# Q loaded in 1 KB runs, and the query order restored by the masking multiply

## The chip, the cores and the metric

One core of one Trainium2 chip. The metric is the device time of one execution in microseconds (us). Each kernel was executed several times; the profile shows one of these executions. A run is called fast or slow by its time and its granted TensorE clock; ratios and intervals below use fast runs alone.

## The reference

Sliding-window causal attention (8 batches, 8 heads, 576 tokens, head size 64, window 64), followed by a gated two-layer network on the 4608 tokens (512 to 2048 to 512):

```python
scores = q @ k.T / sqrt(64)                       # per batch and head
mask   = (rel >= 0) & (rel < 64)                  # rel = query position - key position
attn   = softmax(where(mask, scores, -1e9))
x      = (attn @ v) as [tokens, heads * 64]
h      = x @ w_in
out    = (h * clip(h + 3, 0, 6) / 6) @ w_out
```

q, k and v are fp32 in DRAM, about 0.1 in size. The scores are so small that the softmax is nearly uniform over the window.

## The kernel before

Short names: PV is the product of the probabilities and V, K^T and x^T are transposes that a DMA makes (of K, and of the attention's result x), an `hT` bank is a piece of PSUM that holds one matmul group's result. The code is shortened; `...` marks what is left out.

The work is cut into stages of about 32 us. In stage T the TensorE does the two network layers of 512 tokens (`s1`, then `s2`); between their matmul groups it does the attention of a later batch. A batch has four pairs of heads `g`. For one pair:

```python
def load_blocks(t, src, b, kbs, tail=0):          # token s0 + p on partition p: 256 B runs
    for kb in kbs:
        ...
        nc.sync.dma_start(out=t[p0:p0+ss, kb, :, :],
                          in_=src[b, :, s0:s0+ss, :].rearrange("h s d -> s h d"))

def load_for_dma(b):                              # batches 2 to 7: q, k, v alike
    for n, src in (("qst", q), ("kst", k), ("vst", v)):
        t = stage.tile([P, KB, H, D], F32, name=n, tag=n)
        ins += load_blocks(t, src, b, range(KB), SR if src is v else 0)
...   # GpSimd casts to bf16 (qn, kn, V), then a DMA transpose gives QT, KT [d, token]

def scores(bt, g, u, ...):                        # st: PSUM, keys on partitions
    nc.tensor.matmul(st[:, h, o0:o0+n], lhsT=KT[..., k0:k0+P], rhs=QT[..., q0:q0+n])   # 192 queries per block
    # later: Exp on the ScalarE, PSUM -> SBUF bf16
    nc.scalar.activation(out=pT[:, :, 2*u:2*u+2, 0:QW], in_=st[...], func=EXP, scale=scale)

def masked(bt, g):                                # VectorE, in place, 2 * 4 * 192 = 1536 elements
    nc.vector.tensor_tensor(out=pT[:, :, :, 0:QW], in0=pT[:, :, :, 0:QW], in1=mask, op=MULT)
...   # PV matmuls into two hT banks of PSUM, then reciprocal and multiply (VectorE): opg
```

The VectorE runs in order. Besides the multiply it has the gate of each of the 16 matmul groups of `s1` (`gT`, 0.69 us), which frees the group's PSUM bank, and the normalisation of the PV result (`rec`, `opg`), which frees the two `hT` banks. From batch 3 on, the first two multiplies of a batch stand among the gates:

```python
p1 = {10: [f(SS, 0)], 14: [f(SS, 1)]}             # SS: scores, Exp, multiply of a pair
p2 = {0: [f(SS, 2)], 1: [f(N_, 0)], 3: [f(SS, 3), f(xt_dma, 0)], 4: [f(N_, 1)],
      ..., 7: [f(N_, 2)], ..., 10: [f(N_, 3)], 12: [f(X_, 3)]}   # N_: PV and normalisation
```

The softmax here doesn't subtract the row's maximum and nothing guards it: scores larger than these inputs give would overflow.

## Time and profile before

| | before |
|---|---|
| time, median of 3 | 319.54 us (319.47 to 319.94) |
| span of the profiled run | 317.6 us, granted clock 1.0 |
| TensorE busy | 300.8 us |
| VectorE busy | 173.9 us |
| masking multiply | shortest 947 ns, median 958 ns |

The head of the profile's page. Each engine's busy time, its share of the span and its instructions:

```profile
PE 300.8 (95%) x2131; PEld 149.5 (47%) x2167; DVE 173.9 (55%) x331; ACT 177.9 (56%) x265; POOL 85.7 (27%) x131
```

The waits of the TensorE: engine, line, what was written, who ended the wait, us in total, times, longest.

```profile
PE st L347 <- DMA KT<-kn: 2.4, 2, 2.0
...
PE st L466 <- DMA xT<-opg: 1.0, 1, 1.0
```

So the TensorE is the bound. Of its 16.8 us of idle time (317.6 - 300.8), 3.4 us are waits for transfers in the middle of the kernel; a lighter Q load can win these.

Groups of the page: line, engine, operation, operands, shapes, count, then busy us and mean ns, idle time before.

```profile
L365 DVE TENSOR_TENSOR pT<-pT,mask 128x1536 bf16<-128x1536 bf16 x28 | 28.1, 1004 | 23.0 <-ACT pT L355 23.0
...
L252 POOL CAST qn<-qst 128x512 bf16<-128x512 f32 x24 | 16.1, 712 | 74.1 <-DMA qst<-in_q_dram 59.7
```

The timeline of the VectorE and then of the TensorE in one stage (start, duration, engine, line, operation):

```profile
142.15 0.96 DVE L365 TENSOR_TENSOR pT<-pT,mask 128x1536 bf16<-128x1536 bf16 x1 [0.72 <-ACT pT L355]
143.03 0.68 DVE L474 SCALAR_TENSOR_TENSOR gT<-t,hT 128x512 bf16<-128x512 bf16 x1
...
146.15 0.96 DVE L365 TENSOR_TENSOR pT<-pT,mask 128x1536 bf16<-128x1536 bf16 x1 [0.65 <-ACT pT L355]
147.03 0.68 DVE L474 SCALAR_TENSOR_TENSOR gT<-t,hT 128x512 bf16<-128x512 bf16 x1
```

```profile
144.36 1.04 PE L466 MATMUL hT<-xT,win 128*128 128x512 bf16 x4
...
147.76 0.22 PE L377 MATMUL hT<-V,pT 128*128 128x65 bf16 x2
```

The last gate of the stage starts at 147.03 and ends at 147.71; the PV group that takes the bank it frees starts at 147.76. The engine that looks 45% idle has almost no slack here. Every delay of this gate is a delay of the TensorE.

### The profile page before, as it was taken

The page shows a single profiled execution, that of the slowest core. Times are in us where ns is not written, and L with a number is a line of the kernel's source. Part 1 is how long each engine was busy: PE and PEld are TensorE (multiplying, and loading weights), DVE is VectorE, ACT ScalarE, POOL GpSimd, SP SyncE. Part 2 cuts the span into 40 slices and gives each one's busy share as a digit, 9 for nine tenths or more (in the row PEclk, how much of TensorE's full clock was granted, in tenths as well). Part 3 has the DMA queues.
Part 4 walks back from the last instruction along what each step waited for, and adds up shares of the span by engine and source line. Part 5 has one row for each costly group of instructions (what it writes and reads, how often), then busy time and mean ns, then how long its engine had stood idle before and what let it go on. Part 6 is the DMA issues. An engine that isn't in the chain of part 4 may idle for free.

```text
span 317.6 us, 5604 instructions
## 1 busy us (share of the span) xinstructions
PE 300.8 (95%) x2131; PEld 149.5 (47%) x2167; DVE 173.9 (55%) x331; ACT 177.9 (56%) x265; POOL 85.7 (27%) x131
## 2 busy tenths in 40 slices
PE   8989799999999799899999999999999999999995
PEld 3454345544554355344544554445444544444442
DVE  4658643476636665277527853785378438406700
ACT  2748753387637771487258725872587347417711
POOL 5741805363045143305610650065000000000000
PEclk9999999999999999999999999999999999999999
DMA  8999999999799999999999998999800630010011
GB/s 211 237 173 253 238 199 205 204 184 248 158 208 209 270 215 205 191 254 204 195 257 210 207 184 208 211 201 185 204 34 2 122 75 0 28 73 33 0 68 66
DMA packets 150843, 52.64 MB, mean 166 GB/s; under 512 B 138272, under 2 KB 146464, under 8 KB 150816
## 3 DMA queue, kind: packets, MB, share of 16 engines
q1 hardware_dynamic: 146000, 46.77, 72.7%
q0 software_dynamic: 4544, 5.24, 9.5%
q8 instruction: 17, 0.28, 0.4%
q10 hardware_dynamic: 272, 0.26, 0.2%
q14 instruction: 10, 0.08, 0.1%
HBM read 36.70 MB, written 9.44 MB: 145 GB/s over the span
## 4 chain that ended last, share of the span: by engine, by line
PE 63%; DMA 21%; SPq 8%; POOL 3%; issue 2%; DVE 1%; ACT 1%; POOLq 0%
PE o L503 15%; PE acc L503 14%; PE hT L466 14%; PE acc L466 5%; PE o L466 5%; SPq L94 5%; DMA vst<-in_v_dram 4%; DMA kst<-in_k_dram 4%; DMA KT<-kn 4%; DMA qst<-in_q_dram 3%; PE st L466 3%; PE st L347 3%; DMA wout<-in_moe_w_out_dram 3%; DMA win<-in_moe_w_in_dram 3%; PE hT L377 1%
## 5 line engine op out<-in xcount | busy, mean ns | idle before, releaser
L466 PEld LDWEIGHTS <-win 128*128 128x128 bf16 x576 | 55.3, 98 | 67.2 <-issue 2.3
L503 PEld LDWEIGHTS <-gT 128*128 128x128 bf16 x576 | 52.9, 98 | 57.5 <-issue 0.6
L503 PE MATMUL o<-wout,gT 128*128 128x512 bf16 x274 | 67.5, 379 | 1.5 <-DMA wout<-in_moe_w_out_dram 0.7
L503 PE MATMUL acc<-wout,gT 128*128 128x512 bf16 x278 | 67.1, 379 | 0.7 <-issue 0.3
L466 PE MATMUL hT<-xT,win 128*128 128x512 bf16 x266 | 65.7, 379 | 0.3
L355 ACT ACTIVATE pT<-st 128x768 bf16<-128x768 f32 x64 | 48.9, 813 | 10.8 <-PE st L347 10.7
L473 ACT ACTIVATE t<-hT,half 128x512 bf16<-128x512 f32 x68 | 46.7, 690 | 9.6 <-PE hT L466 9.2
L474 DVE SCALAR_TENSOR_TENSOR gT<-t,hT 128x512 bf16<-128x512 bf16 x68 | 46.4, 685 | 9.4 <-ACT t L473 9.1
L474 DVE SCALAR_TENSOR_TENSOR gT<-t,st 128x512 bf16<-128x512 bf16 (+1 forms) x26 | 19.7, 768 | 52.9 <-ACT t L473 52.9
L365 DVE TENSOR_TENSOR pT<-pT,mask 128x1536 bf16<-128x1536 bf16 x28 | 28.1, 1004 | 23.0 <-ACT pT L355 23.0
L509 ACT COPY osb<-o 128x512 f32<-128x512 f32 x18 | 10.6, 586 | 46.2 <-PE o L503 46.2
L252 POOL CAST qn<-qst 128x512 bf16<-128x512 f32 x24 | 16.1, 712 | 74.1 <-DMA qst<-in_q_dram 59.7
L509 ACT COPY osb<-acc 128x512 f32<-128x512 f32 x18 | 10.6, 587 | 35.7 <-PE acc L503 33.7
L466 PE MATMUL st<-xT,win 128*128 128x512 bf16 x117 | 28.2, 379 | 1.7 <-DMA xT<-opg 1.0
L397 DVE TENSOR_TENSOR opg<-hT,rec 128x320 bf16<-128x320 f32 x56 | 27.5, 492 | 1.9
L466 PE MATMUL acc<-xT,win 128*128 128x512 bf16 x91 | 23.6, 379 | 0.1
L466 PE MATMUL o<-xT,win 128*128 128x512 bf16 x90 | 23.5, 379 | 0.1
L473 ACT ACTIVATE t<-st,half 128x512 bf16<-128x512 f32 (+1 forms) x26 | 19.4, 752 | 7.2 <-PE st L466 7.1
L377 PEld LDWEIGHTS <-pT 128*128 128x128 bf16 x256 | 17.8, 97 | 9.1 <-issue 1.4
L347 PE MATMUL st<-QT,KT 64*128 64x192 bf16 (+2 forms) x320 | 17.9, 229 | 4.2 <-DMA KT<-kn 2.4
L394 DVE RECIPROCAL rec<-hT 128x5 f32<-128x5 f32 x56 | 10.5, 188 | 20.0 <-PE hT L386 19.9
L243 POOL CAST V<-vst 128x512 bf16<-128x512 f32 (+1 forms) x14 | 16.4, 1168 | 17.4 <-DMA vst<-in_v_dram 17.0
(76 smaller groups left out, 269.2 us busy)
## 6 DMA issues: line engine op xcount, KB each, us to landing
out_dram<-osb SPq DMA_DIRECT2D x32, 256.0 KB, 2.4
qst<-in_q_dram SPq DMA_DIRECT2D x28, 256.0 KB, 4.7
kst<-in_k_dram SPq DMA_DIRECT2D x27, 256.0 KB, 5.4
vst<-in_v_dram SPq DMA_DIRECT2D x24, 256.0 KB, 5.1
vst<-in_v_dram SPq DMA_DIRECT2D x24, 128.0 KB, 4.1
win<-in_moe_w_in_dram POOLq DMA_DIRECT2D x4, 512.0 KB, 7.6
wout<-in_moe_w_out_dram POOLq DMA_DIRECT2D x4, 512.0 KB, 8.8
qst<-in_q_dram SPq DMA_DIRECT2D x2, 512.0 KB, 6.1
```

The lines of the kernel that those rows point to most:

```text
L243: copy(out=self.V[:, 0 : KB - 1, h0:h1, 0:D], in_=vst[:, 0 : KB - 1, h0:h1, :])
L252: pcopy(out=n[:, g, 0 : KB - 1, :, :].rearrange("p k h d -> p k (h d)"), in_=s[:, 0 : KB - 1, 2 * g : 2 * g + 2, :].rearrange("p k h d -> ...
L347: nc.tensor.matmul(st[:, h, o0 : o0 + n], lhsT=bt.KT[h * D : (h + 1) * D, g, k0 : k0 + P], rhs=bt.QT[h * D : (h + 1) * D, g, q0 : q0 + n], ...
L355: nc.scalar.activation(out=pT[:, :, 2 * u : 2 * u + 2, 0:QW], in_=st[:, :, 0:w].rearrange("p h (k w) -> p h k w", k=2), func=EXP, scale=scale,
L365: nc.vector.tensor_tensor(out=pT[:, :, :, 0:QW], in0=pT[:, :, :, 0:QW], in1=mask[:].rearrange("p (h k) w -> p h k w", h=2), op=MULT,)
L377: nc.tensor.matmul(ob, lhsT=pT[:, h, qb, 0:P], rhs=V[:, qb, 2 * g + h, :], start=True, stop=(qb == 0),)
L397: nc.vector.tensor_tensor(out=opgs[bt.b, g][:, :, h, :], in0=ov[:, :, 0:D], in1=rec[:].unsqueeze(2).to_broadcast([P, KB, D]), op=MULT,)
L466: nc.tensor.matmul(hT, lhsT=win16[:, g, fc * P : (fc + 1) * P], rhs=xT[:, g, t0 : t0 + TB], start=(g == 0), stop=(g == NG - 1),)
L473: nc.scalar.activation(out=t1[:], in_=hT, func=RELU, bias=half[:], scale=1.0 / 6.0)
L474: nc.vector.scalar_tensor_tensor(out=out, in0=t1[:], scalar=1.0, in1=hT, op0=MIN, op1=MULT,)
L503: nc.tensor.matmul(accs[ts], lhsT=gT[:, fc, ts * P : (ts + 1) * P], rhs=wout16[:, fc, :], start=(fc == 0), stop=(fc == NFC - 1),)
L509: nc.scalar.copy(out=osb[:], in_=accs[ts])
```

## The change

Q of batches 2 to 7 is loaded with four neighbouring tokens to a partition: runs of 1 KB in place of 256 B (the first 512 tokens; the last 64 are loaded as before). The transposed Q then comes with its queries in the order (j, s) for token 4 s + j. The score matmuls read it in four short runs and leave the scores in the order (j, s) too; the Exp writes them to a new tile `raw`; and the multiply, which has to read and write all of it anyway, writes its result at the place of token 4 s + j, that is 2-byte elements in steps of 8 B. The intent is to relieve the transfers and to get the reordering for nothing. In the shortened diffs, a pattern in quotes behind a tile stands for its `rearrange`.

```diff
 def load_for_dma(b):
+    for h0 in range(0, H, 4):
+        nc.sync.dma_start(out=qst[:, h0:h0+4, :],
+            in_=q[b, h0:h0+4, 0:SM, :].rearrange("h (p j) d -> p h (j d)", j=R))
+    nc.sync.dma_start(out=rst[0:SR, :, :], in_=q[b, :, SM:S, :].rearrange("h s d -> s h d"))
-    for n, src in (("qst", q), ("kst", k), ("vst", v)):
+    for n, src in (("kst", k), ("vst", v)):
 ...                                    # cast: qn in the order (j, h, d) of a partition's tokens
 def scores(...):                       # batches 2 to 7
+    matmul(st[...]"(j s) -> j s"[:, :, 0:n], lhsT=KT[...], rhs=QT[...]"(j s) -> j s"[:, :, s0:s0+n])
+    activation(out=raw[:, :, 2*u:2*u+2, :], in_=st[...], func=EXP, scale=scale)
 def masked(bt, g):
+    nc.vector.tensor_tensor(
+        out=pT[:].rearrange("p h k (s j) -> p (h k) j s", j=R)[:, :, :, 0 : QW // R],
+        in0=raws.pop((bt.b, g))[:].rearrange("p h k (j s) -> p (h k) j s", j=R),
+        in1=maskj[:], op=MULT)
```

More of the change, by code (lines that the diff above doesn't have):

```diff
@@ L56 @@
     stage = ctx.enter_context(tc.tile_pool(name="stage", bufs=1))
+    rawp = ctx.enter_context(tc.tile_pool(name="raw", bufs=2))
     small = ctx.enter_context(tc.tile_pool(name="small", bufs=4))
@@ L125, in load_for_dma @@
         sts, ins = [], []
-        for n, src in (("qst", q), ("kst", k), ("vst", v)):
+        qst = stage.tile([P, H, R * D], F32, name="qst", tag="qst")
+        rst = stage.tile([P, H, D], F32, name="rst", tag="rst")
+        for h0 in range(0, H, 4):
+            ins.append(nc.sync.dma_start(
+                out=qst[:, h0 : h0 + 4, :],
+                in_=q[b, h0 : h0 + 4, 0:SM, :].rearrange("h (p j) d -> p h (j d)", j=R),
+            ))
+        ins.append(nc.sync.dma_start(
+            out=rst[0:SR, :, :], in_=q[b, :, SM:S, :].rearrange("h s d -> s h d"),
+        ))
+        for n, src in (("kst", k), ("vst", v)):
             t = stage.tile([P, KB, H, D], F32, name=n, tag=n)
@@ L129, in load_for_dma @@
             sts.append(t)
-        return tuple(sts), ins
+        return ((qst, rst), *sts), ins
     ctx.enter_context(tc.manual_schedule())
@@ L216 @@
     mask = consts.tile([P, 2 * (KB - 1), QW], BF16, name="mask")
+    maskj = consts.tile([P, 2 * (KB - 1), R, QW // R], BF16, name="maskj")
+    raws = {}
     win16 = consts.tile([P, NG, FF], BF16, name="win16")
@@ L249, in cast_for_dma @@
         def cast_for_dma(self, st, which=(0, 1, 2)):
-            for n, s in [((qn_all, st[0]), (kn_all, st[1]))[i] for i in which if i < 2]:
+            for i in which:
+                if i > 1:
+                    continue
+                n = (qn_all, kn_all)[i]
                 for g in range(NG):
-                    pcopy(
-                        out=n[:, g, 0 : KB - 1, :, :].rearrange("p k h d -> p k (h d)"),
-                        in_=s[:, 0 : KB - 1, 2 * g : 2 * g + 2, :].rearrange("p k h d -> p k (h d)"),
-                    )
+                    if i:
+                        pcopy(
+                            out=n[:, g, 0 : KB - 1, :, :].rearrange("p k h d -> p k (h d)"),
+                            in_=st[1][:, 0 : KB - 1, 2 * g : 2 * g + 2, :].rearrange("p k h d -> p k (h d)"),
+                        )
+                    else:
+                        pcopy(
+                            out=n[:, g, 0 : KB - 1, :, :],
+                            in_=st[0][0][:, 2 * g : 2 * g + 2, :].rearrange("p h (j d) -> p j h d", j=R),
+                        )
+                rest = st[1][:SR, KB - 1, :, :] if i else st[0][1][:SR, :, :]
                 pcopy(
                     out=n[:SR, :, KB - 1, :, :].rearrange("p g h d -> p g (h d)"),
-                    in_=s[:SR, KB - 1, :, :].rearrange("p (g h) d -> p g (h d)", h=2),
+                    in_=rest.rearrange("p (g h) d -> p g (h d)", h=2),
                 )
@@ L340, in scores @@
                 )
+        if bt.b > 1:
+            QJ = QW // R
+            if u == 0:
+                raws[bt.b, g] = rawp.tile([P, 2, KB - 1, QW], BF16, name="raw")
+            for i in range(2):
+                for h in range(2):
+                    kb = 2 * u + i
+                    n = min(QJ, P - kb * P // R)
+                    nc.tensor.matmul(
+                        st[:, h, i * QW : (i + 1) * QW].rearrange("p (j s) -> p j s", j=R)[:, :, 0:n],
+                        lhsT=bt.KT[h * D : (h + 1) * D, g, kb * P : (kb + 1) * P],
+                        rhs=bt.QT[h * D : (h + 1) * D, g, 0:SM].rearrange("d (j s) -> d j s", j=R)[
+                            :, :, kb * P // R : kb * P // R + n
+                        ],
+                        start=True, stop=True,
+                    )
+            if u:
+                for h in range(2):
+                    nc.tensor.matmul(
+                        st[:, h, QW : 2 * QW].rearrange("p (j s) -> p j s", j=R)[:, :, P // R : QJ],
+                        lhsT=bt.KT[h * D : (h + 1) * D, g, S - P : S],
+                        rhs=bt.QT[h * D : (h + 1) * D, g, SM:S].rearrange("d (s j) -> d j s", j=R),
+                        start=True, stop=True,
+                    )
+            raw = raws[bt.b, g]
+            return lambda: nc.scalar.activation(
+                out=raw[:, :, 2 * u : 2 * u + 2, :],
+                in_=st[:, :, 0:w].rearrange("p h (k w) -> p h k w", k=2),
+                func=EXP, scale=scale,
+            )
         blocks = (
@@ L364, in masked @@
         pT = P_ring[(bt.b * NG + g) % NPT]
+        if bt.b > 1:
+            nc.vector.tensor_tensor(
+                out=pT[:].rearrange("p h k (s j) -> p (h k) j s", j=R)[:, :, :, 0 : QW // R],
+                in0=raws.pop((bt.b, g))[:].rearrange("p h k (j s) -> p (h k) j s", j=R),
+                in1=maskj[:], op=MULT,
+            )
+            return
         nc.vector.tensor_tensor(
@@ L746, in pieces @@
         return p1, p2
+    nc.vector.tensor_copy(out=maskj[:], in_=mask[:].rearrange("p n (s j) -> p n j s", j=R))
     bt2 = Batch(2)
```

## The prediction

> **What bounds the kernel now.** The TensorE. The page has it busy 300.8 of 317.6 us at full clock. In 8 us windows it idles about 0.05 us each from 136 us on. Its waits after 50 us add up to about 5 us; those that transfers end are K^T of batch 3 (2.0 us at 105 us, timeline), x^T of batch 3's last pair (1.0 us at 130 us) and K^T of batch 2 (0.4 us at 76 us). So a lighter Q load can win about 3.4 us.
>
> **What the change removes.** Q of six batches: 4096 runs of 256 B become 1024 runs of 1 KB per batch. In the sync queue's timeline the five Q issues of a batch take 4.2 to 6.0 us, and from 47 to 133 us the queue is never free. I estimate 1.5 to 2.5 us saved per batch; twice that is ahead of batch 3's K^T, which was 2.0 us late. All three waits should go: -3.4 us.
>
> **What it adds.** The masking multiply (24 of 28) writes 2-byte elements 8 bytes apart. The Trainium skill, "VectorE: DVE Perf Modes", "The perf-mode tier table", gives tensor_tensor in bf16 from SBUF 2x, and its section on that mode asks for step 1. The trace agrees: 1536 elements in 958 ns. At one element a cycle I estimate 1.75 us (gate ops in the trace: 512 elements 685 ns, 320 in 492 ns, slope 1.0 ns). +0.8 us each, 19 us of VectorE time, VectorE from 174 to about 194 us. Exp, GpSimd casts and score matmuls keep their durations.
>
> **How much is on the path.** Read in the timelines of the stage at 139 to 160 us, per stage of batches 3 to 7:
> - first multiply 0.8 longer: the four gates behind it slip, the bank that the last gate matmul group needs is freed 0.1 to 0.2 us late;
> - second multiply: the last gate of the stage ended 0.1 us before the second PV group of pair 0 took its bank; now it is about 0.7 us late;
> - fourth multiply: normalisation of pair 1 behind it is late for PV of pair 2 by about 0.4 us.
> Together about 1.2 us, five stages: +6 us. Batch 2 has slack: 0. The multiply has two SBUF inputs and already stretched to 1.36 us beside GpSimd casts; longer multiplies collide more: +0 to 1 us.
>
> Sum: 319.5 - 3.4 + 6 + 0.5 = 322.6 us. 80% range 318.3 to 331. Chances: faster by over 2% 0.02, within 2% 0.78, slower by over 2% 0.20.
>
> **What would show it.** Groups: the multiply at 1.7 to 1.8 us; q1 packets down by 18,400; VectorE busy up 19 to 20 us. Waits: TensorE no longer waits for K^T or x^T transfers (over 0.3 us), but for VectorE (gates releasing hT banks, reciprocal/normalisation) about 1.2 us in each of five stages, at the last gate group, PV of pair 0 and PV of pair 2. TensorE busy unchanged within 1 us.
>
> **What would make it wrong.** If strided 2-byte writes cost more than one cycle[...], the multiply takes 2.5 to 4 us, the time 335 or more; a memset of 40 elements 130 bytes apart took 92 ns against 59 ns for one, which speaks against it. If the multiply keeps the 2x rate, the time is 316. If the earlier transfers move GpSimd's 1.9 us V cast onto a multiply, stages lose more than I say.

## The result, and the profile after

| | before | after |
|---|---|---|
| time | 319.74 us median of 4 | 370.42 us median of 4 (368.04 to 373.66) |
| ratio of fast runs | | 1.154, 95% interval 1.144 to 1.164 |
| span, granted clock of the profiled run | 317.6 us, 1.0 | 371.9 us, 0.967 |
| TensorE busy | 300.8 us | 316.1 us |
| VectorE busy | 173.9 us | 241.1 us |
| masking multiply, batches 2 to 7 | 0.96 us | shortest 3.57, mean 3.92, longest 5.67 us |

A ratio here is the mean time of one kernel's fast runs over that of the other's of the same rounds, so not quite the ratio of the medians. The profiled run of after was its slowest (373.66 us); its fast runs were 368 to 371.7 us at a clock of 0.977 to 0.986. So its waits are read here, but its clock is a little lower than usual, and the fast profiles of e2 and e9 below are taken to confirm it.

The page of after, and the group of the multiply:

```profile
PE 316.1 (85%) x2131; PEld 152.6 (41%) x2167; DVE 241.1 (65%) x332; ACT 177.9 (48%) x265; POOL 120.6 (32%) x131
...
L419 DVE TENSOR_TENSOR pT<-raw,maskj 128x1536 bf16<-128x1536 bf16 x24 | 93.8, 3917 | 9.7 <-ACT raw L389 9.7
...
L274 POOL CAST qn<-qst 128x512 bf16<-128x512 f32 x24 | 20.8, 894 | 83.5 <-DMA qst<-in_q_dram 83.5
```

Waits of the TensorE:

```profile
PE hT L437 <- DVE gT L534: 12.2, 5, 2.9
PE hT L437 <- DVE opg L457: 12.2, 13, 2.6
PE hT L526 <- DVE gT L534: 9.6, 5, 2.1
PE hT L467 <- DVE opg L457: 3.6, 3, 1.7
...
PE hT L437 <- DVE pT L419: 1.4, 1, 1.4
...
PE st L372 <- DMA KT<-kn: 0.6, 1, 0.6
```

These five waits for the VectorE are 39.0 us. 34.0 us are in the stages of batches 3 to 7, at the kinds of place that the prediction named: the last gate group of a stage (L526) and the PV groups (L437). New are the transpose of the result (L467, 3.6 us) and the 1.4 us that end with the multiply itself: both are in the stage of batch 2, from 84 to 99 us, for which the prediction had 0. The transfer waits went from 3.4 us to 0.6. The packets of the hardware queue fell by 18,624 (146,000 to 127,376), as the prediction had it.

The span grew by 54.3 us: 39.0 us more idle TensorE, and 15.3 us more busy TensorE. About 10 us of the second part are the granted clock; what the other 5 us are was not taken apart (both traces have 2131 matmul records where e1 to e3 have 2167, so the sums are short by a little). The stretch of one stage, in windows of 4 us (PE, PEld, DVE, ACT and POOL busy, then PEclk, the DMA share and GB/s):

```profile
160.00:164.00 4.00, 3.13 (x22) 1.39 (x22) 3.57 (x6) 3.12 (x5) 3.04 (x5) 1.00 1.19 212
164.00:168.00 4.00, 1.20 (x18) 0.94 (x18) 4.00 (x3) 0.95 (x2) 4.00 (x3) 0.79 0.55 103
168.00:172.00 4.00, 3.95 (x18) 1.56 (x18) 4.00 (x1) 0.72 (x2) 3.94 (x2) 0.50 0.00 0
172.00:176.00 4.00, 3.81 (x29) 1.75 (x30) 3.91 (x6) 1.28 (x2) 1.66 (x2) 0.85 0.58 103
```

In the second window the TensorE was busy for 1.2 of 4 us, and in the third it ran at half clock. Over the whole span I sum busy time times (1 - clock) in such windows: 10.0 us for after, 0.0 for before. The Trainium skill, "TensorE: Matmul & The Clock Gate", "What's actually happening", says that the clock is halved after an idle window of about 3.4 us. This trace has half clock behind long waits, but the longest of its waits is 2.95 us, so none was as long as that window. Here there were two waits, of 2.05 us (to 160.84) and 2.63 us (to 167.23), with 3.8 us of work between them. The length of the waits does not decide it alone: one stage later two waits of 1.82 and 2.60 us (to 202.56 and 208.92) left the clock at 1.0, as the single 1.97 us wait of before did, while in e7 a single wait of 2.34 us was followed by half clock. No run here shows the rule.

The timeline of the VectorE in this stage, and the second PV group that waits for its gate:

```profile
163.00 3.66 DVE L419 TENSOR_TENSOR pT<-raw,maskj 128x1536 bf16<-128x1536 bf16 x1 [0.43 <-ACT raw L389]
166.46 0.72 DVE L534 SCALAR_TENSOR_TENSOR gT<-t,hT 128x512 bf16<-128x512 bf16 x1
167.11 5.66 DVE L419 TENSOR_TENSOR pT<-raw,maskj 128x1536 bf16<-128x1536 bf16 x1
```

```profile
167.23 0.27 PE L437 MATMUL hT<-V,pT 128*128 128x65 bf16 x2 [2.63 <-DVE gT L534]
```

It is the pair of lines shown of before at 147.03 and 147.76: gate, then PV. The gate is now 2.7 us late because the multiply in front of it takes 3.66 us in place of 0.96.

GpSimd at the same time:

```profile
161.51 5.44 POOL L269 CAST kn<-kst 128x512 bf16<-128x512 f32 x4 [0.96 <-DMA kst<-in_k_dram]
166.89 0.60 POOL L279 CAST kn<-kst 64x512 bf16<-64x512 f32 x1
167.45 1.89 POOL L256 CAST V<-vst 128x2048 bf16<-128x2048 f32 x1
169.40 3.65 POOL L257 CAST V<-vst 64x512 bf16<-64x512 f32 x1
```

Four K casts that take 0.61 us each by themselves took 5.44 us, the multiply at 167.11 took 2.1 us more than the shortest while the 1.89 us V cast ran, and the small V cast (0.61 us by itself) took 3.65 us and ended 0.3 us after that multiply. The Trainium skill, "SBUF — State Buffer", "Who interferes with whom", says that a VectorE instruction with two SBUF inputs and a GpSimd instruction that reads SBUF block each other, whichever is second. The trace agrees.

### The profile page after: what moved, and what is told of

Its sections match the earlier page's. It is cut to its first block, busy times and chain, and to the rows that moved or that the text cites. A ratio compares the mean times of both kernels' runs of the same rounds, so it can differ in the third digit from the quotient of the medians.

```text
span 371.9 us, 5575 instructions
## 1 busy us (share of the span) xinstructions
PE 316.1 (85%) x2131; PEld 152.6 (41%) x2167; DVE 241.1 (65%) x332; ACT 177.9 (48%) x265; POOL 120.6 (32%) x131
## 3 DMA queue, kind: packets, MB, share of 16 engines
q1 hardware_dynamic: 127376, 46.77, 58.3%
## 4 chain that ended last, share of the span: by engine, by line
PE 46%; DVE 25%; DMA 11%; ACT 8%; issue 5%; POOL 3%; SPq 1%; ACTq 0%; POOLq 0%
DVE pT L419 19%; PE o L563 11%; PE acc L563 11%; PE hT L526 8%; ACT raw L389 5%; PE st L526 4%; PE acc L526 4%; PE o L526 4%; DVE gT L534 3%; DVE opg L457 3%; DMA wout<-in_moe_w_out_dram 3%; DMA win<-in_moe_w_in_dram 2%; DMA kst<-in_k_dram 2%; ACT t L533 2%; DMA KT<-kn 2%
## 5 line engine op out<-in xcount | busy, mean ns | idle before, releaser
L419 DVE TENSOR_TENSOR pT<-raw,maskj 128x1536 bf16<-128x1536 bf16 x24 | 93.8, 3917 | 9.7 <-ACT raw L389 9.7
L526 PEld LDWEIGHTS <-win 128*128 128x128 bf16 x576 | 55.5, 98 | 76.8 <-issue 10.5
L563 PEld LDWEIGHTS <-gT 128*128 128x128 bf16 x576 | 55.0, 101 | 64.2 <-issue 11.1
L563 PE MATMUL o<-wout,gT 128*128 128x512 bf16 x274 | 74.4, 409 | 2.3 <-DMA wout<-in_moe_w_out_dram 1.0
L526 PE MATMUL hT<-xT,win 128*128 128x512 bf16 x266 | 65.6, 379 | 9.9 <-DVE gT L534 9.6
L563 PE MATMUL acc<-wout,gT 128*128 128x512 bf16 x278 | 69.4, 389 | 0.7 <-issue 0.3
L274 POOL CAST qn<-qst 128x512 bf16<-128x512 f32 x24 | 20.8, 894 | 83.5 <-DMA qst<-in_q_dram 83.5
L437 PE MATMUL hT<-V,pT 128*128 128x65 bf16 x224 | 18.4, 197 | 26.3 <-DVE gT L534 12.2
L389 ACT ACTIVATE raw<-st 128x768 bf16<-128x768 f32 x48 | 36.2, 814 | 4.4 <-PE st L372 4.4
L269 POOL CAST kn<-kst 128x512 bf16<-128x512 f32 x24 | 28.0, 1206 | 18.8 <-DMA kst<-in_k_dram 18.8
L437 PEld LDWEIGHTS <-pT 128*128 128x128 bf16 x256 | 17.9, 98 | 39.2 <-DVE opg L457 16.7
L569 ACT COPY osb<-acc 128x512 f32<-128x512 f32 x18 | 10.5, 586 | 44.5 <-PE acc L563 42.6
L526 PE MATMUL st<-xT,win 128*128 128x512 bf16 x117 | 28.1, 379 | 1.6 <-DMA win<-in_moe_w_in_dram 1.0
L526 PE MATMUL acc<-xT,win 128*128 128x512 bf16 x91 | 23.6, 379 | 0.1
L526 PE MATMUL o<-xT,win 128*128 128x512 bf16 x90 | 23.5, 379 | 0.1
```

The costliest lines, as they stand in the source:

```text
L269: pcopy(out=n[:, g, 0 : KB - 1, :, :].rearrange("p k h d -> p k (h d)"), in_=st[1][:, 0 : KB - 1, 2 * g : 2 * g + 2, :].rearrange("p k h d ...
L274: pcopy(out=n[:, g, 0 : KB - 1, :, :], in_=st[0][0][:, 2 * g : 2 * g + 2, :].rearrange("p h (j d) -> p j h d", j=R),)
L389: return lambda: nc.scalar.activation(out=raw[:, :, 2 * u : 2 * u + 2, :], in_=st[:, :, 0:w].rearrange("p h (k w) -> p h k w", k=2), func= ...
L419: nc.vector.tensor_tensor(out=pT[:].rearrange("p h k (s j) -> p (h k) j s", j=R)[:, :, :, 0 : QW // R], in0=raws.pop((bt.b, g))[:].rearran ...
L437: nc.tensor.matmul(ob, lhsT=pT[:, h, qb, 0:P], rhs=V[:, qb, 2 * g + h, :], start=True, stop=(qb == 0),)
L526: nc.tensor.matmul(hT, lhsT=win16[:, g, fc * P : (fc + 1) * P], rhs=xT[:, g, t0 : t0 + TB], start=(g == 0), stop=(g == NG - 1),)
```

## The experiments

My theory after the result (theory 1): the whole loss is the multiply's duration on the VectorE, from the strided write; the load, the matmuls and the new tile are innocent. Rivals: a part of it comes from moved transfers and casts or from the matmuls (A); the loss of two elements a cycle is enough by itself, with the collisions (B, D); any pattern that isn't innermost-dense costs as much (C).

### e1: the multiply writes densely

```diff
-    out=pT[:].rearrange("p h k (s j) -> p (h k) j s", j=R)[:, :, :, 0 : QW // R], ...
+    out=pT[:, :, :, 0:QW].rearrange("p h k w -> p (h k) w"),
+    in0=raw "p h k w -> p (h k) w", in1=maskj "p n j s -> p n (j s)"      # wrong order, on purpose
```

> The changed kernel with one edit: the multiply writes its result densely (query order not restored, so the result is wrong on purpose). Theory 1 (the whole loss is the multiply's duration on the VectorE): the multiply is back at 0.95 to 1.0 us, the GpSimd casts near 0.61 us, the TensorE waits for the VectorE gone, time 316 to 318 us, that is 1.5 to 3.5 us under the kernel before. Rival A (part of the loss is elsewhere: score matmuls that read four short runs, the extra tile between Exp and multiply, transfers or casts that now come at other times): the time stays above 325 us with the multiply at 1 us.

Measured: ratio to before 0.993 (interval 0.986 to 1.001). Two runs at a clock of 0.998 or more took 316.4 and 316.9 us; the other two, at 0.992 and 0.989, took 320.5 and 322.3 (the last is left out of the ratio). The profiled one, 320.5 us, has a dip of the clock near 42 us. The multiply, and the largest wait for the VectorE from 60 us on (1.6 us in all):

```profile
L419 DVE TENSOR_TENSOR pT<-raw,maskj x24: 957/959/2647, 80.0 to 248.9; 128x1536 bf16<-128x1536 bf16 x24
PE hT L437 <- DVE opg L457: 1.3, 3, 0.9
```

Rival A falls: with new load, new matmul patterns and new tile the loss is gone. The gain of 1.5 to 3.5 us that was expected is not clear of the noise in these runs. The wrong result was found by the check (the mask no longer fits).

### e2: the old load, the new multiply

```diff
-    (Q in 1 KB runs, cast in the order j h d)
+    (Q loaded and cast as before)              # scores, raw, strided multiply as after; wrong on purpose
```

> The changed kernel with Q loaded and cast as before (256 B runs); score matmuls, Exp, multiply with 8 B steps as after; wrong result on purpose, mask read from the unpermuted tile. Theory 1: 366 to 376 us, as the changed kernel, multiply 3.6 us in its shortest runs; the load takes part neither in the loss nor, now, in any gain, as the stages wait for the VectorE. Rival A (moved transfers and casts make the loss): 320 to 345 us.

Measured: ratio 1.167 (1.163 to 1.172), 372.9 to 374.8 us. Waits for the VectorE 42.6 us from 60 us on, clock 0.963; the multiply and the largest of the waits:

```profile
L398 DVE TENSOR_TENSOR pT<-raw,mask x24: 3569/3598/5589, 77.8 to 301.1; 128x1536 bf16<-128x1536 bf16 x24
PE hT L416 <- DVE gT L513: 15.1, 5, 4.4
```

So the loss is all there without the new load, and rival A falls again. e2 is 1.3% slower than after (1.167 against 1.154), which would mean that the new load still wins something, against the expectation; but the two ran on different chips and their intervals overlap, so this stays open. This is also a fast profile with the clock as low as in the one of after.

### e3: one element a cycle, no steps

```diff
+    mask32 = consts.tile([P, KB - 1, QW], F32)
-    (strided multiply with the bf16 mask)
+    nc.vector.tensor_tensor(out=pT[:, :, :, 0:QW], in0=raw[:],
+        in1=mask32[:].unsqueeze(1).to_broadcast([P, 2, KB - 1, QW]), op=MULT)   # wrong order, on purpose
```

> The changed kernel with a dense multiply whose mask is fp32 (result wrong on purpose): one element a cycle, no steps. This is the multiply that the prediction assumed. Theory 1: 1.75 us each, and, if the prediction's path was right (3.4 us won, 6 to 7 us lost), 321 to 325 us; if the stages have more slack than it read, 316 to 319. Rival B (one element a cycle is already enough for the measured loss, e.g. because of collisions with GpSimd): above 340 us.

This is the kernel that the prediction thought it was looking at. Measured: multiply shortest 1748 ns, median 1760; ratio 1.028 (1.023 to 1.033), 328.1 to 328.8 us in the three runs at a clock of 0.998 or more (330.8 us in the profiled one, at 0.992). So the estimate of 1.75 us for one element a cycle was right, and it is a loss of only 8 to 9 us. Rival B falls. But the time is also 6 us above the 322.6 that the prediction made of this duration; e8 takes that apart. The waits for the VectorE (8.5 us from 60 us on):

```profile
PE hT L436 <- DVE gT L533: 4.8, 5, 1.2
PE hT L436 <- DVE opg L456: 3.4, 9, 1.1
```

### e4: eight forms of the multiply in one kernel

```diff
+    v = ((bt.b - 2) * NG + g) % 8      # three multiplies of each form; wrong on purpose
+    0: dense    1: dense, fp32 mask
+    2, 3, 4, 5: out=pT "p h k (s j) -> p (h k) j s" with j = 2, 4, 8, 16   # steps of 4, 8, 16, 32 B
+    6: out dense, in0=raw "(j s) -> s j"     # read in steps of 96 B: restores the order
+    7: out dense, in0=raw "(s j) -> j s"     # read in steps of 8 B
```

> The changed kernel with eight forms of the multiply in turn, three of each (result wrong on purpose): dense; dense with fp32 mask; write steps of 4, 8, 16, 32 B; dense write with a read of one input in steps of 96 B (which restores the order); dense write with a read in steps of 8 B. Theory 1a (a step costs what the short run of 2-byte writes costs the memory port, over the loss of two elements a cycle): shortest dense 0.95, fp32 1.75, 4 B 1.75, 8 B 3.6, 16 and 32 B 3.6 to 4, read in steps of 96 B 2.5 to 3.9. Rival C (any pattern that isn't innermost-dense, or any pattern in short rows, costs 3.6 us): 4 B also 3.6, and the reads too. Rival D (only the loss of two elements a cycle plus contention): all 1.75.

Measured, in the order of the forms 0 to 7 (shortest/median/longest ns):

```profile
L429 DVE TENSOR_TENSOR pT<-raw,mask x3: 957/958/958, 77.9 to 239.0; 128x1536 bf16<-128x1536 bf16 x3
L431 DVE TENSOR_TENSOR pT<-raw,mask x3: 1759/1759/1760, 79.3 to 243.1; 128x1536 bf16<-128x1536 bf16 x3
L433 DVE TENSOR_TENSOR pT<-raw,mask x3: 1900/2241/2253, 82.4 to 245.3; 128x1536 bf16<-128x1536 bf16 x3
L435 DVE TENSOR_TENSOR pT<-raw,mask x3: 3957/4839/4874, 86.3 to 249.7; 128x1536 bf16<-128x1536 bf16 x3
L437 DVE TENSOR_TENSOR pT<-raw,mask x3: 6984/6986/6995, 107.9 to 276.7; 128x1536 bf16<-128x1536 bf16 x3
L439 DVE TENSOR_TENSOR pT<-raw,mask x3: 6639/6641/7128, 117.6 to 286.5; 128x1536 bf16<-128x1536 bf16 x3
L441 DVE TENSOR_TENSOR pT<-raw,mask x3: 2737/3391/5105, 125.1 to 293.5; 128x1536 bf16<-128x1536 bf16 x3
L447 DVE TENSOR_TENSOR pT<-raw,mask x3: 1749/1759/1759, 131.4 to 299.7; 128x1536 bf16<-128x1536 bf16 x3
```

The 8 B form fell beside GpSimd casts in all three places (two of them beside a V cast of 1.90 us); after and e2 have it at 3569 ns alone. Rivals C and D fall: a read in steps of 8 B takes 1.76 us, as the dense form with the fp32 mask does, while a write in steps of 8 B takes more than twice that. The rows get shorter as the steps of the writes get longer (96, 48, 24 and 12 elements), so the length of a row was not held; but the read in steps of 8 B has rows of 48 too, and rows of 12 took no longer than rows of 24. My own sizes for 16 and 32 B (3.6 to 4 us) were wrong by a factor of almost two, and 4 B took 1.90 us where I had 1.75.

Take 158 ns off (what the dense form leaves over 768 cycles at the 0.96 GHz that the Trainium skill, "VectorE: DVE Perf Modes", "Specifications", gives): the writes cost 1.09, 2.13, 4.27 and 4.05 cycles an element at steps of 4, 8, 16 and 32 B. At 4, 8 and 16 B, where four, two and one element fall into each 16 B of SBUF, that is 4.3 to 4.4 cycles for every 16 B touched; at 32 B it is 4.05. The numbers fit a cost for each 16 B piece written in part; no run here shows the mechanism.

### e5: four other places for the reordering

```diff
-    (raw tile and strided multiply)
+    multiply in place and dense; v = (bt.b + g) % 4 chooses where the order is restored:
+    0: activation(out=pT dense, in_=st "(j s) -> s j")     # Exp reads PSUM in steps of 192 B
+    1: activation(out=pT "(s j) -> j s", in_=st dense)     # Exp writes SBUF in steps of 8 B
+    2: matmul(out=st "(s j) -> j s", ...)                  # PSUM written in steps of 16 B
+    3: matmul(..., rhs=QT "(j s) -> s j")                  # moving operand in steps of 256 B
```

For an Exp in one instruction, pT was laid out as [u, h, k] and the PSUM blocks start at multiples of 256.

> The changed kernel with the multiply dense again (in place, two elements a cycle) and the query order restored at four other places in turn, six pairs each: (0) Exp reads PSUM in steps of 192 B and writes densely; (1) Exp reads densely and writes in steps of 8 B; (2) the score matmul writes PSUM in steps of 16 B; (3) the score matmul reads its moving operand in steps of 256 B. Right result by construction. If the 16 B line cost of the last runs holds for any engine that writes SBUF, (1) takes the Exp from 0.81 to over 1.7 us; if it is the VectorE's own, 0.81. (0): 0.81 if PSUM reads in steps are free, else 1 to 2 us. (2) and (3): a pair of ten score matmuls takes 0.5 us now; free means 0.5, a cost per element means 1 us and more. Whichever form leaves all four durations alone is the one for a whole kernel, at 316 to 317 us. Multiply 0.95 to 1.0 us in all.

Measured: the Exp of the forms 0 and 1, and the ten score matmuls of a pair with the plain pattern and in the forms 2 and 3:

```profile
L392 ACT ACTIVATE pT<-st x12: 802/811/817, 83.0 to 253.7; 128x768 bf16<-128x768 f32 x12
L397 ACT ACTIVATE pT<-st x12: 1876/1934/1983, 86.9 to 256.6; 128x768 bf16<-128x768 f32 x12
```

```profile
176.97 0.53 PE L383 MATMUL st<-QT,KT 64*128 64x192 bf16 x10
...
211.86 0.82 PE L385 MATMUL st<-QT,KT 64*128 64x192 bf16 x10
...
247.41 1.39 PE L387 MATMUL st<-QT,KT 64*128 64x192 bf16 x10
```

So this strided write to SBUF is dear on the ScalarE too (1.93 us against 0.81), and both TensorE forms cost time on the engine that bounds the kernel (0.82 to 0.90 us and 1.39 us for a pair, against 0.53). The Exp's strided read of PSUM costs nothing (0.81 us in both). (Single run, correct, 333 us: the four forms mixed.)

### e6 and e7: the free place, with the new and with the old load

e6 is form 0 of e5 for all pairs, with the multiply dense and in place. e7 is the same with Q loaded and cast as before (its query order is wrong).

> The changed kernel with the query order restored by the Exp, which reads PSUM in steps of 192 B, and the multiply dense and in place as before. Right result by construction. Theory 1: Exp 0.81 us, multiply 0.95 to 1.0 us where no cast collides, casts near 0.61 us; the TensorE waits for K^T and x^T transfers are gone; 315.5 to 317.5 us in runs at full clock, 1% faster than before (less in the mean if runs with a dip of the granted clock are among them). Rival: earlier transfers and casts collide with multiplies enough to give the 3 us back: 319 to 321 us.

Measured: ratio 0.993 (0.990 to 0.997), 317.2 to 319.5 us beside 319.5 to 322.9 for before on that chip. Exp 0.81 us, multiply median 959 ns; no wait for a transfer is left after 60 us. The two runs at full clock took 317.2 and 319.4 us, so only one of them is within the 315.5 to 317.5 us that I expected. 0.7% better than before is the best correct version found. Its correctness rests on the index maps and on the mask, since the check doesn't see the query order.

> The same kernel with Q loaded and cast as before the change (256 B runs), so the query order comes out wrong on purpose. It separates the load from the new layout of scores and probabilities. Theory 1 (the load is the whole gain): 319 to 320.5 us, with the TensorE waits for K^T and x^T transfers (2 us and 1 us) back. Rival (the new layout wins or loses by itself): over 1.5 us away from the kernel before.

Measured: ratio 1.002 (0.997 to 1.006). One wait for a transfer is back, for K^T of batch 3 (2.3 us); the one for x^T is not:

```profile
107.74 0.71 PE L363 MATMUL st<-QT,KT 64*128 64x192 bf16 x10 [2.34 <-DMA KT<-kn]
...
108.00:112.00 4.00, 4.00 (x19) 1.58 (x16) 1.65 (x2) 2.44 (x4) 0.00 (x0) 0.59 1.13 260
```

(The second line is the window behind that wait, in the columns used above: its granted clock is 0.59, and 0.50 from 108 to 110 us.) So the layout is neutral within the noise, and the new load is worth 0.8%, or 2.7 us: 1.0016 - 0.9932 = 0.0084, times 319.5. From the two intervals I estimate plus or minus 1.7 us.

### e8 and e9: without the casts

```diff
-    p1.setdefault(12 if T == 1 else 6, []).append(lambda bt=nxt, sts=sts: bt.cast_for_dma(sts))
```

This takes the GpSimd casts of batches 3 to 7 away, so that these use old data (wrong): e8 from e3, e9 from after.

> e3 (dense multiply with fp32 mask, 1.76 us) without the GpSimd casts of batches 3 to 7 (so those batches use old data: wrong on purpose, if the check can see it). Nothing is left on GpSimd that a multiply could collide with. If collisions with casts are what made e3 slower than the prediction's path said, all multiplies of batches 3 to 7 take 1.75 us, each stage waits 1.0 to 1.2 us for the VectorE as batch 7 did in e3, and the time falls from 328 to 322 to 325 us. If the path itself was read too short (refills of the TensorE, small waits), it stays at 327 or above.

Measured: all multiplies 1748 to 1759 ns; ratio 1.020 (1.016 to 1.024), 325.3 to 327.9 us. Neither of the two answers alone: the collisions are about 0.8% (1.028 - 1.020; 2.6 us, plus or minus 2 us by the two intervals, the two ratios being of different chips), and the path was read too short as well. Waits for the VectorE:

```profile
PE hT L436 <- DVE gT L533: 4.0, 5, 0.8
...
PE hT L436 <- DVE opg L456: 1.1, 5, 0.2
```

5.1 us in five stages, 1.0 each, near the 1.2 of the prediction, at two of its three places: 0.8 at PV of pair 0 and 0.2 at PV of pair 2. For the last gate group no wait is listed. Yet the stage is longer by more than that. From the first score group to the first gate group of the next stage, the TensorE's timeline has 22.44 us before (204.00 to 226.44) and 24.41 us in e8 (205.73 to 230.14): 2.0 us. The other 1.0 us is not in the list of waits. Comparing the starts one by one, it is in pauses that the profile counts as busy: the last gate group is 0.2 us later behind its bank, the third pair's scores take 0.2 us more (they follow an Exp that now comes later), and the PV groups of pair 2 start 0.2 us late; each restart also costs about 0.15 us beyond the wait that is listed.

> The changed kernel without the GpSimd casts of batches 3 to 7 (wrong on purpose). Multiplies of these batches all at 3.57 us in place of a mean of 3.9; each stage waits about 6.4 us as batch 7 did; time 362 to 367 us in place of 368 to 372. So the strided write itself would be most of the 50 us and the collisions 3 to 8 us. If collisions were the larger part, it falls below 350.

Measured: 363.7 to 368.5 us, ratio 1.140 (1.134 to 1.146), multiplies 3554 to 3627 ns, waits for the VectorE 34.4 us from 60 us on (39.3 in after), clock 0.976, 7.0 us lost to it by the same sum as above. The three largest waits:

```profile
PE hT L437 <- DVE gT L534: 11.4, 5, 2.6
PE hT L526 <- DVE gT L534: 9.1, 5, 1.8
PE hT L437 <- DVE opg L457: 8.8, 16, 1.7
```

The collisions are 1.4% (1.154 - 1.140), about 5 us of the 49 (plus or minus 4 us by the two intervals, different chips). The strided write itself is the rest: against e8, on the same chip and also without casts, it is 12.0% (1.140 - 1.020).

## Why the prediction was wrong

The direction and the place were right; the size was not, and the time lay far outside the range. Point by point:

- "So a lighter Q load can win about 3.4 us": held within the noise. e6 against e7 gives 2.7 us (plus or minus 1.7), and the two K^T waits and the x^T wait are gone in e6. In e7 only one of the three came back (K^T of batch 3, 2.3 us), so the account by waits is rough.
- "At one element a cycle I estimate 1.75 us": **this is the step that failed.** One element a cycle does take 1.76 us (e3, e4), but the multiply that the change makes doesn't run at one element a cycle. It takes 3.57 us alone and 3.92 in the mean, because of its writes in steps of 8 B (e1, e4). The prediction named this possibility with nearly the right duration, "2.5 to 4 us, the time 335 or more", and set it aside because of a memset of 40 elements 130 B apart that took 92 ns. The rate of that burst of 40 elements did not carry over to a multiply of 1536; why the short one was fast stays open. The Trainium skill, "Vector Engine (DVE) Microarchitecture Reference", "5.2 Measured stream behaviour on trn2", has 2.5 ns a column for a destination that steps 24 words of 4 B in each element, against 1.05 ns dense; that should have weighed more than the memset. No run here has that pattern; the nearest, in e4, has 4.2 ns at 32 B steps of 2-byte elements ((6639 - 158) / 1536).
- "Together about 1.2 us, five stages: +6 us": the listed waits at 1.76 us without collisions were 1.0 us a stage (e8), at two of the three places named; the third, the last gate group, was 0.2 us late without a listed wait. The stage that was compared grew by 2.0 us, since small pauses inside groups are not listed as waits. So this term was 8 to 10 us and not 6: five such stages are 10 us, and e8 is 2.6% or 8.4 us above e1 (1.020 - 0.993, on different chips).
- "+0 to 1 us" for collisions with GpSimd: about 2.6 us at 1.76 us a multiply (e3 against e8), about 5 us at 3.57 (after against e9), both with the wide margins given there.
- "Batch 2 has slack: 0": right at 1.76 us a multiply (e3 and e8 list no wait over 0.3 us before the stage of batch 3), wrong at 3.57, where batch 2 waits for 5.0 us.
- "TensorE busy unchanged within 1 us": wrong, 15.3 us more in the profiled run, of which about 10 us are a lower granted clock, in stretches that follow waits of 1.8 to 3.0 us. e8, with no wait above 0.8 us after 60 us, ran at 0.999.

The sum from the runs, as shares of the time before: the load wins 0.8% (e7 to e6). A dense multiply at one element a cycle costs 3.5% over e1 (1.028 - 0.993), collisions included. The strided write costs 12.6% more (1.154 - 1.028); in the profiles (that of after is its slowest run) it is 39.3 - 8.5 = 31 us of waits for the VectorE and some 8 us of clock (10.0 - 1.8). The loss grows faster than the multiply: each stage has some slack that the first 0.8 us nearly used up. From e8 to e9 each multiply is 1.8 us longer, and the wait at the last gate group goes from none to 1.8 us, at PV of pair 0 from 0.8 to 2.6 (1.2 in the stage of batch 3), at PV of pair 2 from 0.2 to between 0.9 and 1.7. So from there on nearly every microsecond of the first and second multiply, and a large part of the fourth, is one of the TensorE.

## What to carry to other kernels

Don't scatter 2-byte results in SBUF: a write in steps of 8 B cost 2.1 cycles an element where a dense one cost 0.5, while an Exp that read PSUM in steps of 192 B cost nothing. So try a reordering on the read side of an instruction first, and measure it there: a multiply that read SBUF in steps of 96 B took 2.74 us against 0.96 dense. An engine that is 55% busy may still have no slack at the one instruction that frees a PSUM bank, so look at the gap between that release and its taker before adding to the engine's queue. And take a rate only from an instruction of about the same length and pattern, or measure it by itself first; eight forms in one kernel took a single run.

## What the Trainium skill lacked or had wrong

- "SBUF — State Buffer", "Door 1: The DMA port swizzle (why `[64,N]` ≈ `[32,N]`)", says that SBUF lines are 16 B, that at least two hits to a line give full bandwidth, and that one can stride for free as far as 8 bf16. For reads it held: steps of 8 B (two hits) ran at 1759 ns, one cycle an element. For writes of the VectorE it did not: steps of 8 B took 3569 ns, of 16 B 6984 ns, of 4 B 1900 ns, about 4.3 cycles for each 16 B.
- "Vector Engine (DVE) Microarchitecture Reference", 5.2: its strided rows are for 4-byte words. Missing are 2-byte destinations in steps of 4, 8, 16 and 32 B: 1.09, 2.13, 4.27 and 4.05 cycles an element; and a 2-byte source in steps of 96 B: 2737 ns for 1536 elements where nothing collided, 1.6 cycles.
- No page gives the ScalarE's strided costs: Exp of 768 elements 811 ns with PSUM read in steps of 192 B, as dense; 1934 ns with SBUF written in steps of 8 B.
- "SBUF — State Buffer", the same section, says that non-contiguous PSUM patterns slow matmuls significantly. It agrees, and here is a size: ten score matmuls 0.53 us dense, 0.82 us with PSUM written in steps of 16 B; 1.39 us with the moving operand read in steps of 256 B (of SBUF, so not a case of that sentence).
- "TensorE: Matmul & The Clock Gate", "What's actually happening", ties the half clock to an idle window of about 3.4 us. In the trace of after six stretches at half clock followed waits of 1.76 to 2.95 us, none as long as that window; in e7 one followed a single wait of 2.34 us. Like waits were not followed by one: 2.26 us (to 136.09) and 1.82 and 2.60 us (to 202.56 and 208.92) in after, 1.97 us in before. e1, e3, e6 and e7 also had dips near 42 us, and e6 one near 22 us, that no run here explains.
